# A short convolution on eight 64-row by 32-column tiles, fed by a shifted copy of its input made on chip

## The chip, the cores and the metric

The kernel runs on one core of a Trainium2 chip. The metric is the device time of one execution in microseconds (us), the median of several runs. A run is called slow when it is over 1.5% above the fastest run of the same kernel. Ratios are the mean time of one kernel's fast runs over that of the other's fast runs of the same rounds, so they are not quite the ratio of the medians that are quoted beside them.

The engines are named as in the profile: PE is TensorE (matmuls), PEld its weight loads, DVE is VectorE, ACT is ScalarE, POOL is GpSimd, SP is the engine that only issues DMAs here. "PEclk" is the TensorE clock that was granted, as a share of full speed.

## The reference

```python
# x: (8, 4224, 192), weight: (8 heads, 7 taps)
w = softmax(weight, axis=-1)
y[b, s, h*24:(h+1)*24] = sum_k w[h, k] * x_pad[b, s + k, h*24:(h+1)*24]   # causal, 6 zero rows ahead
h = (y.transpose(0, 2, 1) @ U @ V).transpose(0, 2, 1)                      # mixing over tokens, rank 32
u = y + h
out = u + relu(u @ w_ch1) @ w_ch2                                          # 192 -> 768 -> 192
```

So every output token needs its own input row and the six rows before it, per head, with a small band matrix.

## The kernel before

The input of a batch lies in one tile `x_sb`. Partitions 0 to 63 hold the first half of the batch's 66 blocks of 64 tokens, partitions 64 to 127 the second half; each half has the block ahead of it as well, for the taps that reach back.

```python
    def x_part(b, r, s0, s1):                    # one of four loads of a batch, float32 to bf16, POOL's queue
        blk = NB0 * r + s0 - 1
        return nc.gpsimd.dma_start(
            out=xt[b][HB * r : HB * r + HB, s0:s1, :],
            in_=x[b, blk * HB : (blk + s1 - s0) * HB, :].rearrange("(j p) d -> p j d", p=HB),
        )
    # ...
    def conv(b, h0, nh, rs, engs, k0=0, k1=NT):  # HB = 64, GS = 24 columns of a head
        # ...
        for hh in range(nh):
            h = h0 + hh
            for halo in range(2):                # this block, then the block before it
                for r in rs:
                    for c in range(2):           # even and odd blocks: the two halves of the output
                        st = 1 - halo + c + 2 * k0
                        nc.tensor.matmul(
                            out=pp[r][HB * c : HB * c + HB, ...],
                            lhsT=band[HB * r : HB * r + HB, h, HB * halo : HB * halo + HB],
                            rhs=xt[b][HB * r : HB * r + HB, st : st + 2 * nk[r] - 1 : 2, h * GS : h * GS + GS],
                            start=(halo == 0), stop=(halo == 1),
                            tile_position=(HB * r, HB * c),
                        )
        # ... then one eviction of pp[r] (PSUM) to y_sb for each r, on ACT or DVE
```

A head thus costs eight matmuls on 64x64 tiles and two evictions (128x384 and 128x408). Four run at a time: at the start of a conv in the trace of the kernel before, four start within 10 ns (125.365 to 125.375 us) and the next four 0.18 us later (from 125.551). The second four are the halo products, most of whose band is zero.

The main loop is a row of stretches. Each has W1 (`relu(u @ w_ch1)`, line L518) of three groups of eight token tiles, then the conv of a batch or part of one, then twelve W2 pieces (L542), between which the mixing products for later groups are put (`h`: add the rank-32 part to y; then a DMA transpose `uT` on SP's queue for a later W1).

```python
    CONV = {
        5: [(3, 0, 8)], 6: [(4, 0, 8)], 7: [(5, 0, 4)],
        8: [(5, 4, 8), (6, 0, 3)], 9: [(6, 3, 8), (7, 0, 2)], 10: [(7, 2, 8)],
    }   # stretch: (batch, first head, end)
    # ...
    for gs1, gs2, convs, at in SLOTS:
        for g in gs1:
            ends = w1(g, RELU0 if g < 2 else RELU)
            # ... x loads of a later batch, held back until given W1 products
        for b, h0, h1 in convs:
            for h in range(h0, h1):
                conv(b, h, 1, [0, 1], "AD" if n > 2 else "A")
        for p in range(npc + 1):
            for what in at.get(p, []):
                do(what)                          # h group, its transpose, sums over tokens
            # ... one W2 piece, its eviction on DVE, its output DMA on SP's queue
```

## Time and profile before

| | |
|---|---|
| time | 336.25 us median of 3 (334.5 to 336.35) |
| PE busy | 97% of a span of 332.2 us |
| DVE, ACT busy | 84%, 48% |
| conv of batches 1 to 7 in the chain | 22.3 us, 56 heads |

Three lines of the page of the kernel before: PE's busy time, and over 40 slices of the span the granted clock and the busy share of the DMA engines in tenths.

```profile
PE 323.7 (97%) x4072; PEld 226.9 (68%) x4072; DVE 280.3 (84%) x571; ACT 159.2 (48%) x327; POOL 38.0 (11%) x63
...
PEclk9999999999999999999999999999999999999999
DMA  8999994799999899899699695069049239439135
```

PE is busy for 97% of the span, and the mean granted clock is 1.000.

The chain of waits of the kernel before, one stretch with a conv of eight heads (start, duration, what):

```profile
125.44 3.30 PE ps L309 x61
128.74 2.09 PE ps L542 x24
130.82 0.28 PE ps L424 x8
131.10 4.07 PE ps L542 x48
```

Only PE pieces: the conv (L309) is 3.30 us, on the critical path. The timeline of the same place shows why it is 3.30 and not less:

```profile
125.36 3.37 PE L309 MATMUL ps<-x_sb,band 64*64 64x384 bf16 x64
125.96 3.19 ACT L271 ACTIVATE y_sb<-ps 128x384 bf16<-128x384 f32 x8
126.11 4.00 DVE L273 CAST y_sb<-ps 128x408 bf16<-128x408 f32 x8
```

ACT and DVE evict from start to end, eight times each, about 0.5 us apiece; PE outruns them after five heads and then waits for banks: the last three heads start at 127.226, 127.716 and 128.206 us, each 0.05 us after one of DVE's evictions has ended (127.173, 127.662 and 128.152).

The stretch table of the kernel before, for four stretches (the last column but one is the DMA share: the time of all packets over 16 engines times the stretch; above 1 means that the times of packets overlap):

```profile
core 0: us, PE busy (x) PEld busy (x) DVE busy (x) ACT busy (x) POOL busy (x), PEclk, DMA share, GB/s
113.67:142.88 29.21, 29.21 (x378) 20.24 (x379) 25.42 (x54) 14.64 (x30) 3.53 (x5) 1.00 1.02 182
142.88:169.36 26.48, 26.48 (x311) 18.34 (x312) 23.79 (x46) 12.78 (x25) 3.55 (x5) 1.00 1.09 186
169.36:198.16 28.80, 28.80 (x369) 20.07 (x371) 25.36 (x52) 14.26 (x29) 3.35 (x4) 1.00 1.04 177
198.16:226.96 28.80, 28.80 (x369) 20.10 (x371) 25.68 (x55) 14.26 (x29) 0.00 (x0) 1.00 0.53 137
```

The first three stretches load a batch of x (POOL issues) and have DMA shares of 1.02 to 1.09. The fourth loads none: 0.53.

SP's timeline of the kernel before, near the conv of batch 1, which PE reaches at 40.4 us:

```profile
36.63 2.28 SPq L465 DMA_TRANSPOSE uT<-u_sb  x1
38.95 2.01 SPq L557 DMA_DIRECT2D out_dram<-out_sb  x2
```

### The profile page before, as it was taken

The page shows a single profiled execution, that of the slowest core. Times are in us where ns is not written, and L with a number is a line of the kernel's source. Part 1 is how long each engine was busy: PE and PEld are TensorE (multiplying, and loading weights), DVE is VectorE, ACT ScalarE, POOL GpSimd, SP SyncE. Part 2 cuts the span into 40 slices and gives each one's busy share as a digit, 9 for nine tenths or more (in the row PEclk, how much of TensorE's full clock was granted, in tenths as well). Part 3 has the DMA queues.
Part 4 walks back from the last instruction along what each step waited for, and adds up shares of the span by engine and source line. Part 5 has one row for each costly group of instructions (what it writes and reads, how often), then busy time and mean ns, then how long its engine had stood idle before and what let it go on. Part 6 is the DMA issues. An engine that isn't in the chain of part 4 may idle for free.

```text
span 332.2 us, 9693 instructions
## 1 busy us (share of the span) xinstructions
PE 323.7 (97%) x4072; PEld 226.9 (68%) x4072; DVE 280.3 (84%) x571; ACT 159.2 (48%) x327; POOL 38.0 (11%) x63
## 2 busy tenths in 40 slices
PE   7889999999999999999999999999999999999995
PEld 7745675578559747955965884695597487488495
DVE  5757999989898889899888898889898889887863
ACT  1658436650790295068049209605902921922910
POOL 8471110210210030021012000000000000000000
PEclk9999999999999999999999999999999999999999
DMA  8999994799999899899699695069049239439135
GB/s 102 193 160 186 139 235 118 136 199 256 200 188 134 231 188 166 186 203 199 183 202 194 107 235 139 19 180 234 2 73 278 81 83 255 94 80 251 54 119 169
DMA packets 122909, 53.55 MB, mean 161 GB/s; under 512 B 87760, under 2 KB 122832, under 8 KB 122864
## 3 DMA queue, kind: packets, MB, share of 16 engines
q1 hardware_dynamic: 84672, 38.18, 49.1%
q0 software_dynamic: 38192, 14.73, 39.2%
q8 instruction: 32, 0.52, 0.6%
q14 instruction: 13, 0.11, 0.1%
HBM read 29.49 MB, written 25.95 MB: 167 GB/s over the span
## 4 chain that ended last, share of the span: by engine, by line
PE 88%; DMA 3%; ACT 3%; POOL 2%; DVE 2%; issue 0%; POOLq 0%
PE ps L542 41%; PE ps L518 37%; PE ps L309 6%; PE ps L424 3%; DMA x_sb<-in_x_dram 3%; ACT rl_sb L529 2%; PE ps L339 2%; DVE y_sb L273 1%; DMA V_sb<-in_moe_V_dram 1%; POOL x_sb L78 1%; DVE rl_sb L531 1%; PE ps L395 0%; POOL V_sb L152 0%; DVE uT L273 0%; POOL Ur L129 0%
## 5 line engine op out<-in xcount | busy, mean ns | idle before, releaser
L529 ACT ACTIVATE rl_sb<-ps 128x512 bf16<-128x512 f32 x235 | 125.2, 605 | 104.9 <-PE ps L518 83.6
L542 PE MATMUL ps<-W_sb,rl_sb 128*128 128x192 bf16 x1584 | 138.9, 246 | 0.0
L542 PEld LDWEIGHTS <-rl_sb 128*128 128x128 bf16 x1584 | 128.7, 98 | 8.9 <-issue 8.8
L518 PE MATMUL ps<-uT,W_sb 64*128 64x512 bf16 x1188 | 131.5, 376 | 0.8 <-DVE uT L273 0.8
L531 DVE TENSOR_SCALAR rl_sb<-ps 128x512 bf16<-128x512 f32 x161 | 105.6, 689 | 19.7 <-PE ps L518 19.3
L518 PEld LDWEIGHTS <-W_sb 64*128 64x128 bf16 x1188 | 57.8, 94 | 70.1 <-issue 4.3
L550 DVE TENSOR_TENSOR out_sb<-ps,u_sb 128x384 f32<-128x384 f32 (+1 forms) x133 | 69.5, 548 | 15.8 <-PE ps L542 15.5
L446 DVE TENSOR_TENSOR u_sb<-y_sb,ps 128x192 bf16<-128x192 bf16 (+1 forms) x168 | 66.2, 460 | 0.0
L78 POOL DMA_DIRECT2D x_sb<-in_x_dram x32 | 27.0, 848 | 134.9 <-PE ps L518 123.1
L273 DVE CAST y_sb<-ps 128x408 bf16<-128x408 f32 (+2 forms) x66 | 32.4, 560 | 2.3 <-PE ps L309 2.3
L309 PE MATMUL ps<-x_sb,band 64*64 64x408 bf16 (+4 forms) x576 | 26.8, 313 | 0.2 <-DMA x_sb<-in_x_dram 0.2
L271 ACT ACTIVATE y_sb<-ps 128x384 bf16<-128x384 f32 (+2 forms) x66 | 26.0, 522 | 1.4 <-PE ps L309 1.2
L309 PEld LDWEIGHTS <-band 64*64 64x64 bf16 x576 | 18.0, 106 | 9.1 <-issue 7.4
L353 ACT ACTIVATE tt_hi<-ps 128x192 bf16<-128x192 f32 x7 | 2.3, 330 | 41.1 <-PE ps L339 41.1
L424 PE MATMUL ps<-tt_sb,V_sb 32*128 32x192 bf16 x264 | 12.1, 246 | 0.2 <-DVE y_sb L273 0.2
L172 PE MATMUL ps<-zz 128*128 128x128 bf16 x90 | 7.6, 266 | 1.2 <-DVE zz L167 1.2
L424 PEld LDWEIGHTS <-V_sb 32*128 32x128 bf16 x264 | 4.5, 92 | 6.3 <-issue 5.8
L172 PEld LDWEIGHTS <-zz 128*128 128x128 bf16 x90 | 7.3, 124 | 1.2 <-DVE zz L167 1.2
L339 PE MATMUL ps<-y_sb,U_sb 128*32 128x192 bf16 x257 | 7.2, 247 | 0.0
L339 PEld LDWEIGHTS <-U_sb 128*32 128x32 bf16 x257 | 5.4, 96 | 1.2 <-issue 1.1
L354 DVE TENSOR_TENSOR tt_lo<-ps,tt_hi 128x192 bf16<-128x192 f32 x7 | 2.5, 356 | 3.9 <-ACT tt_hi L353 3.9
L239 ACT ACTIVATE band<-ps 32x152 bf16<-32x152 f32 x8 | 2.3, 288 | 3.1 <-PE ps L230 3.0
(57 smaller groups left out, 45.1 us busy)
## 6 DMA issues: line engine op xcount, KB each, us to landing
out_dram<-out_sb SPq DMA_DIRECT2D x131, 192.0 KB, 2.8
x_sb<-in_x_dram POOLq DMA_DIRECT2D x14, 384.0 KB, 7.9
x_sb<-in_x_dram POOLq DMA_DIRECT2D x7, 432.0 KB, 9.5
x_sb<-in_x_dram POOLq DMA_DIRECT2D x7, 408.0 KB, 9.6
x_sb<-in_x_dram POOLq DMA_DIRECT2D x1, 648.0 KB, 9.5
x_sb<-in_x_dram POOLq DMA_DIRECT2D x1, 624.0 KB, 7.2
uT<-u_sb SPq DMA_TRANSPOSE x31, 4.2
W_sb<-in_moe_w_ch_dram POOLq DMA_DIRECT2D x2, 192.0 KB, 6.3
```

The costliest lines, as they stand in the source:

```text
L78: return nc.gpsimd.dma_start(out=xt[b][HB * r : HB * r + HB, s0:s1, :], in_=x[b, blk * HB : (blk + s1 - s0) * HB, :].rearrange("(j p) d -> ...
L271: nc.scalar.activation(out=out, in_=in_, func=ACT.Copy)
L273: nc.vector.tensor_copy(out=out, in_=in_)
L309: nc.tensor.matmul(out=pp[r][HB * c : HB * c + HB, 0 : nk[r] * w].rearrange("p (k a) -> p k a", a=w)[:, :, hh * GS : hh * GS + GS], lhsT=b ...
L339: nc.tensor.matmul(out=p[32 * c : 32 * c + 32, o : o + D], lhsT=U_sb[:, j // 4, j % 4, :], rhs=yt[b][:, j, :], start=(n < 4), stop=(n + 4 ...
L424: nc.tensor.matmul(out=banks[pr][:, a * D : (a + 1) * D], lhsT=V_sb[32 * q : 32 * q + 32, (j // 8) * 2 + j % 2, :], rhs=ttb[b][32 * q : 32 ...
L446: nc.vector.tensor_tensor(out=u_group(g)[:, i : i + n, :, hf, :], in0=yt[b][:, run[0] : run[0] + n, :].rearrange("p n (c k) -> p n c k", c=3),
L518: last = nc.tensor.matmul(out=pp[hf][:], lhsT=W1_sb[HB * hf : HB * hf + HB, c, m * P : (m + 1) * P], rhs=uTt[g][HB * hf : HB * hf + HB, :, ...
L529: nc.scalar.activation(out=rl[:, m, hf, :], in_=pp[hf][:], func=ACT.Relu)
L531: nc.vector.tensor_scalar_max(out=rl[:, m, hf, :], in0=pp[hf][:], scalar1=0.0)
L542: nc.tensor.matmul(out=cps[:, a * D : (a + 1) * D], lhsT=rlt[g][:, m, hf, (i + a) * P : (i + a + 1) * P], rhs=W2_sb[:, m, :], start=(m == ...
L550: nc.vector.tensor_tensor(out=o[:, 0:n, :].rearrange("p n (c k) -> p n c k", c=3), in0=cps[:, 0 : n * D].rearrange("p (n c k) -> p n c k", ...
```

## The change

Its intent: drop the halo products. If a second tile `xb_sb` holds the same tokens shifted by 32, then 64 rows of either tile hold 32 output tokens together with the 32 tokens before them, so one product with 64 rows and 32 output columns gives them without any halo. `x_sb` gives the odd 32-token blocks, `xb_sb` the even ones. Eight such tiles cover the 128 by 128 that one W2 product takes (128*128 in the profile's forms, 64*32 for these). The shifted tile is made on chip by four DMAs of 32 partitions each, SBUF to SBUF, on SP's queue. The conv is cut into chunks of two or three heads that stand between W2 pieces, so that evictions have time.

```diff
-    xs = ctx.enter_context(tc.tile_pool(name="xs", bufs=3))
+    xs = ctx.enter_context(tc.tile_pool(name="xs", bufs=2))
+    xbs = ctx.enter_context(tc.tile_pool(name="xbs", bufs=1))
...
+    def x_shift(b):
+        xbt[b] = xbs.tile([P, NB1, D], BF16, name="xb_sb")
+        q = [slice(QB * r, QB * r + QB) for r in range(4)]
+        for dst, src, n in ((2, 1, NB0), (0, 3, NB1)):
+            nc.sync.dma_start(out=xbt[b][q[dst], 0:n, :], in_=xt[b][q[src], 0:n, :])
+            nc.sync.dma_start(out=xbt[b][q[dst + 1], 0:n, :], in_=xt[b][q[src - 1], 1 : n + 1, :])
+
+    def conv32(b, h0, nh, engs):
...
+            for c in range(2):
+                for src in range(2):
+                    for r in range(2):
+                        t, o, cg = ((xt[b], 1, 2 * c + 1), (xbt[b], 0, 2 * c))[src]
+                        part = (r, 1 - r)[src]
+                        st = o + c
+                        nc.tensor.matmul(
+                            out=pp[part][QB * cg : QB * cg + QB, 0 : nk[part] * GS],
+                            lhsT=band[HB * r : HB * r + HB, h, QB : 2 * QB],
+                            rhs=t[HB * r : HB * r + HB, st : st + 2 * nk[part] - 1 : 2, hs],
+                            start=True, stop=True,
+                            tile_position=(HB * r, QB * cg),
+                        )
... (two evictions a head, as before; "AAD" is the turn of ACT and DVE)
-        ([1], [0], [], {0: ["h0"], 1: ["h3"]}),
-        ([2], [1], [(1, 0, 8)], {0: ["h1"], 1: ["t1"], 3: ["s1"], 4: ["h4"]}),
+        ([1], [0], {0: ["h0"], 1: ["h3", "x1"]}),           # x1: the shift of batch 1, before W2 piece 1
+        ([2], [1], {0: ["c1:0:3:AAD", "h1"], 1: ["c1:3:3:AD"], 2: ["c1:6:2:AD"],
+                    3: ["t1"], 4: ["s1", "h4", "x2"]}),
... (batches 2 and 3 likewise)
+        elif k < 10:                                       # stretches 6 to 9, batches 4 to 7
+            hp = (5, 8, 11)
+            put(0, f"c{k - 2}:0:2:AAD")
+            put(1, f"c{k - 2}:2:3:AD")
+            put(2, f"c{k - 2}:5:3:AD")
+            put(8, f"s{k - 2}")
...
+        if k < 9:
+            put(12, f"x{k - 1}")                           # the next batch's shift, at the stretch's end
```

More of the change, by code (lines that the diff above doesn't have):

```diff
@@ L293, in u_layout @@
             )
+    xbt = [None] * B
+    def x_shift(b):
[5 more added lines that the diff above has]
+    def conv32(b, h0, nh, engs):
+        if yt[b] is None:
+            yt[b] = ys.tile([P, NT, D], BF16, name="y_sb")
+        nk = (NB0 // 2, NB1 // 2)
+        for n in range(nh):
+            h = h0 + n
+            hs = slice(h * GS, h * GS + GS)
+            pp = [bank(), bank()]
+            for c in range(2):
[8 more added lines that the diff above has]
+                            rhs=t[HB * r : HB * r + HB, st : st + 2 * nk[part] - 1 : 2, hs],
+                            start=True,
+                            stop=True,
+                            tile_position=(HB * r, QB * cg),
+                        )
+            for part in range(2):
+                j0 = NB0 // 2 * part
+                evac(
+                    engs[(2 * n + part) % len(engs)],
+                    yt[b][:, j0 : j0 + nk[part], hs],
+                    pp[part][:, 0 : nk[part] * GS].rearrange("p (k a) -> p k a", a=GS),
+                )
     def conv(b, h0, nh, rs, engs, k0=0, k1=NT):
@@ L387, in tt_done @@
     def tt_done(b, p):
-        t = sml.tile([P, D], BF16, name="tt_sb")
+        t = sml.tile([P, D], BF16, name="tt_sb", bufs=3)
         nc.vector.tensor_copy(out=t[:], in_=p[:, 0:D])
@@ L570 @@
     SLOTS = [
-        ([0], [], [], {}),
-        ([1], [0], [], {0: ["h0"], 1: ["h3"]}),
-        ([2], [1], [(1, 0, 8)], {0: ["h1"], 1: ["t1"], 3: ["s1"], 4: ["h4"]}),
-        ([3], [2], [(2, 0, 4)], {1: ["h5"]}),
+        ([0], [], {}),
+        ([1], [0], {0: ["h0"], 1: ["h3", "x1"]}),
+        (
+            [2],
+            [1],
+            {
+                0: ["c1:0:3:AAD", "h1"],
+                1: ["c1:3:3:AD"],
+                2: ["c1:6:2:AD"],
+                3: ["t1"],
+                4: ["s1", "h4", "x2"],
+            },
+        ),
+        ([3], [2], {1: ["h5"]}),
         (
@@ L577 @@
             [3, 4, 5],
-            [(2, 4, 8)],
-            {1: ["t2", "h6"], 3: ["s2"], 4: ["h7"], 7: ["h8"], 10: ["h9"]},
-        ),
-    ]
-    CONV = {
-        5: [(3, 0, 8)],
-        6: [(4, 0, 8)],
-        7: [(5, 0, 4)],
-        8: [(5, 4, 8), (6, 0, 3)],
-        9: [(6, 3, 8), (7, 0, 2)],
-        10: [(7, 2, 8)],
-    }
-    SUMS = {5: (3, 5), 6: (4, 10), 8: (5, 2), 9: (6, 6), 10: (7, 10)}
+            {
+                0: ["c2:0:2:AAD"],
+                1: ["c2:2:3:AD", "h6"],
+                2: ["c2:5:3:AD"],
+                4: ["t2", "h7"],
+                6: ["s2"],
+                7: ["h8"],
+                10: ["h9"],
+                12: ["x3"],
+            },
+        ),
+    ]
     nh = 10
@@ L594, with put @@
         at = {}
-        for p in (1, 5, 9) if k == 5 else (2, 6, 10):
+        def put(p, *what):
+            at.setdefault(p, []).extend(what)
+        if k == 5:
+            hp = (6, 9, 11)
+            put(0, "c3:0:3:AD")
+            put(2, "c3:3:3:A")
+            put(7, "c3:6:2:AAD")
+            put(11, "s3")
+        elif k < 10:
[4 more added lines that the diff above has]
+            put(8, f"s{k - 2}")
+        else:
+            hp = (0, 4, 8)
+        for p in hp:
             if nh < NG:
-                at.setdefault(p, []).append(f"h{nh}")
+                put(p, f"h{nh}")
                 nh += 1
-        if k in SUMS:
-            b, p = SUMS[k]
-            at.setdefault(p, []).insert(0, f"t{b}")
-            at.setdefault(p + 2, []).insert(0, f"s{b}")
-        SLOTS.append((gs, gs, CONV.get(k, []), at))
+        if k < 10:
+            put(hp[k == 5], f"t{k - 2}")
+        if k < 9:
+            put(12, f"x{k - 1}")
+        SLOTS.append((gs, gs, at))
     assert nh == NG
-    LOADS = {2: [(1, 5), (1, 5), (2, 2), (2, 5)]}
-    for b, g in ((3, 4), (4, 6), (5, 9), (6, 12), (7, 15)):
+    LOADS = {2: [(1, 5), (1, 5), (2, 2), (2, 5)], 3: [(4, 1), (4, 4), (5, 1), (5, 4)]}
+    for b in range(4, B):
+        g = 3 * b - 6
         LOADS[b] = [(g, 1), (g, 4), (g + 1, 1), (g + 1, 4)]
-    def held(ins, after):
-        tc.add_manual_dep(
-            ins.ins,
-            after.ins.name,
-            mybir.DependencyInfo(mybir.DependencyClass.Sync, mybir.DependencyReason.DATA),
-            reason="load held back",
-        )
     idle(30, P)
@@ L641, in do @@
     def do(what):
+        if what[0] == "c":
+            b, h0, n, engs = what[1:].split(":")
+            conv32(int(b), int(h0), int(n), engs)
+            return
         n = int(what[1:])
@@ L646, in do @@
                 transp(n)
+        elif what[0] == "x":
+            x_shift(n)
         elif what[0] == "t":
@@ L650, in do @@
             tt_sum(n)
-    for gs1, gs2, convs, at in SLOTS:
+    for gs1, gs2, at in SLOTS:
         for g in gs1:
@@ L664 @@
                 do("h2")
-        n = sum(h1 - h0 for _, h0, h1 in convs)
-        for b, h0, h1 in convs:
-            for h in range(h0, h1):
-                conv(b, h, 1, [0, 1], "AD" if n > 2 else "A")
         npc = 4 * len(gs2)
```

## The prediction

> **What bounds the kernel now.** TensorE. The page's busy table has PE at 97%, DVE 84%, ACT 48%. From 33 us on the chain of waits is an almost unbroken run of PE pieces: W2 (L542) 41% of the span, W1 (L518) 37%, conv (L309) 6%. W2 costs 0.083 us per matmul, W1 0.109. So saved PE time is saved time, unless a new wait replaces it.
>
> **What the conv costs.** Batches 1 to 7 are 56 heads. In the chain, four heads take 1.50 us, eight take 3.30; the pieces add up to about 22.3 us. The timeline shows about 0.345 us per head while banks are free (8 matmuls, 43 ns each), then 0.49 per head, because DVE needs 0.572 us for each 128x408 eviction and ACT 0.535 for 128x384.
>
> **What the change removes.** The halo products are half of the array work. [...] Nearest in this trace is the four-column product with U: 33 matmuls in 0.85 us, 26 ns each. Eight at that rate is 0.21 us per head, 11.5 us for 56. Each of 21 chunks pays perhaps 0.12 us to enter and 0.06 on the next W2 piece: 3.5 us together, about 0.5 of it paid before. Conv gain: about 8 us. Evictions are as many and as large; DVE loses one a batch (7 of 16).
>
> **What it adds.**
> 1. Seven shifts of 1.6 MB on SP's queue. Later ones have a W1 stretch (11.8 us) to land in, and should just fit. The first has not: it comes after the transpose that SP issues at 36.6 us and holds for 2.3, so no earlier than 38.9 us, while the conv of batch 1 is reached at 40.4. The DMA row is full there and transfers take 6.9 us to land: landing about 45 to 48 us, an estimate. PE must stand still some 5 us (3 to 8), once, on the critical path.
> 2. The sum for batch 1 now directly precedes the h group that needs it, no W2 piece between; the same for batch 3. With DVE behind by a microsecond or two: about 1.5 us for both.
> 3. In stretches of three groups with a conv, DVE works 26.4 of 29.3 us now. Shorter by 1.3 us, with nearly the same DVE work and an h group just before W1, late evictions will hold banks: about 0.4 us in each of five, 2 us.
>
> **Sum.** -8 + 5 + 1.5 + 2 = about 0.5 us. I predict 335.8 us, range 328 to 343. Chance faster by over 2%: 0.20; within 2%: 0.65; slower by over 2%: 0.15.
>
> **What would show it.** Still eight conv matmuls per head, but with starts about 26 ns apart instead of 43. One PE idle gap of several us near 40 us, released by the shift's DMA. Small PE gaps at W1 starts and before the h groups of batches 1 and 3, released by DVE. DVE share unchanged or higher.
>
> **What would make it wrong.** If the first shift lands by 42 us, the result is nearer 331. [...] If later shifts are late too, several more stalls, above 343.

No term of the sum is cut; it stands at about 0.5 us, and the 0.21 us per head rests on the 26 ns of the products with U. The terms are estimates. The 0.12 us to enter a chunk is 1.50 us for four heads less four times 0.345. The 0.06 us on the next W2 piece, the 1.5 us and the 2 us are guesses that no trace shows; beside the last stands DVE's 26.42 us of work in the 29.28 us from 84.39 us.

## The result, and the profile after

The changed kernel took 397.58 us (median of 4, 397.45 to 405.75; the last of them slow), against 336.29 us for the kernel before (median of 4). The ratio is 1.184, with a 95% interval of 1.179 to 1.189: 18% slower. The prediction of 335.8 us, range 328 to 343, was wrong.

The page after, the lines that answer to those of before:

```profile
PE 329.5 (83%) x4072; PEld 222.8 (56%) x4072; DVE 276.4 (70%) x561; ACT 165.5 (42%) x337; POOL 37.9 (10%) x63
...
PEclk9999759968999699979968997999999999999999
DMA  9999984998799969998999899699384792927425
```

PE fell from 97% to 83% of the span, and the clock row has six dips.

PE's waits after (who waited for whom: us in total, times, the longest):

```profile
PE ps L324 <- DMA xb_sb<-x_sb: 44.3, 6, 13.1
PE ps L562 <- DMA uT<-u_sb: 11.9, 1, 11.9
PE ps L468 <- DVE tt_sb L433: 1.3, 3, 0.6
```

Nothing like the first two lines was there before. Six of the seven convs waited for their shift, 44.3 us in all, in order 13.1, 6.7, 5.5, 8.9, 7.6 and 2.6; and one W1 (L562) waited 11.9 us for a transpose that SP issued right behind a shift, at 74.8 us, and that landed 14.0 us later. Two loads of x ran beside it.

The chain of waits after, through one shift (pieces left out are waits of under 0.1 us and SP's output issue):

```profile
150.61 2.09 PE ps L562 x18
152.71 0.28 SPq L509
...
153.81 0.54 SPq L305
...
154.41 0.59 SPq L306
...
155.11 1.72 SPq L305
...
156.87 11.21 DMA xb_sb<-x_sb
...
168.13 0.87 PE ps L324 x11
```

W1 begins at 150.61 and takes 11.8 us. The shift's first piece is issued only at 153.81, since SP waits for the last output and transpose; the fourth is issued at 156.87 and lands 11.2 us later, at 168.1. PE is ready for it at 162.3.

The stretch table after, from W1 start to W1 start, for the stretches that answer to the four shown of before:

```profile
core 0: us, PE busy (x) PEld busy (x) DVE busy (x) ACT busy (x) POOL busy (x), PEclk, DMA share, GB/s
150.60:186.80 36.20, 30.72 (x378) 20.14 (x379) 24.98 (x52) 15.38 (x31) 3.52 (x5) 0.91 1.06 178
186.80:225.57 38.77, 29.86 (x378) 19.61 (x379) 25.57 (x52) 15.39 (x31) 3.53 (x5) 0.87 1.13 178
225.57:263.05 37.48, 29.88 (x378) 19.57 (x379) 25.57 (x51) 15.39 (x31) 3.35 (x4) 0.91 1.05 183
263.05:293.93 30.88, 28.30 (x378) 18.89 (x379) 25.57 (x55) 15.38 (x31) 0.00 (x0) 1.00 0.73 169
```

Multiply the length of a stretch by its DMA share, and one has the DMA time that it holds. Before it was 29.8, 28.9 and 30.0 us for the three stretches with x loads, about as much as the stretches were long. After it is 38.4, 43.8 and 39.4 us, and the stretches grew by 7.0, 12.3 and 8.7 us. The fourth stretch, without a load, had 15.3 us and got 22.5, and grew by 2.1. (Overlapping packets are counted twice in such a product; it is a load and not a capacity.)

The DMA issues after (count, size, median us from issue to landing), first the shift's pieces, then loads of x:

```profile
xb_sb<-x_sb SPq DMA_DIRECT2D x14, 408.0 KB, 11.1
xb_sb<-x_sb SPq DMA_DIRECT2D x14, 384.0 KB, 8.0
x_sb<-in_x_dram POOLq DMA_DIRECT2D x7, 432.0 KB, 15.6
x_sb<-in_x_dram POOLq DMA_DIRECT2D x7, 408.0 KB, 16.6
```

The same loads before:

```profile
x_sb<-in_x_dram POOLq DMA_DIRECT2D x7, 432.0 KB, 9.5
x_sb<-in_x_dram POOLq DMA_DIRECT2D x7, 408.0 KB, 9.6
```

The loads became 6 to 7 us later as well: both sides lose.

Where the 63.5 us between the two spans (332.2 and 395.7) went, worked out from the trace's records: PE's idle time after 30 us grew by 57.6 us. The granted clock fell to 0.5 in the six gaps of 5.5 us or more and stayed there past their ends; PE was busy for 23.5 us at half clock, so about 11.7 us went there, an estimate. The rest, 5.8 us the other way, is what PE's shorter work saved.

### The profile page after: what moved, and what is told of

Its sections match the earlier page's. It is cut to its first block, busy times and chain, and to the rows that moved or that the text cites. A ratio compares the mean times of both kernels' runs of the same rounds, so it can differ in the third digit from the quotient of the medians.

```text
span 395.7 us, 9752 instructions
## 1 busy us (share of the span) xinstructions
PE 329.5 (83%) x4072; PEld 222.8 (56%) x4072; DVE 276.4 (70%) x561; ACT 165.5 (42%) x337; POOL 37.9 (10%) x63
## 4 chain that ended last, share of the span: by engine, by line
PE 58%; DMA 23%; DVE 10%; SPq 4%; issue 2%; ACT 2%; POOL 0%; DVEq 0%; POOLq 0%
PE ps L586 32%; PE ps L562 18%; DMA xb_sb<-x_sb 17%; PE ps L324 4%; DMA uT<-u_sb 4%; DVE u_sb L490 3%; SPq L305 3%; DMA x_sb<-in_x_dram 3%; DVE out_sb L594 2%; DVE rl_sb L575 2%; PE ps L468 2%; PE ps L383 2%; ACT rl_sb L573 1%; SPq L306 1%; DVE y_sb L274 1%
## 5 line engine op out<-in xcount | busy, mean ns | idle before, releaser
L586 PE MATMUL ps<-W_sb,rl_sb 128*128 128x192 bf16 x1584 | 145.9, 252 | 0.1
L562 PE MATMUL ps<-uT,W_sb 64*128 64x512 bf16 x1188 | 132.7, 379 | 12.6 <-DMA uT<-u_sb 11.9
L586 PEld LDWEIGHTS <-rl_sb 128*128 128x128 bf16 x1584 | 133.0, 100 | 14.8 <-issue 14.0
L562 PEld LDWEIGHTS <-W_sb 64*128 64x128 bf16 x1188 | 58.0, 95 | 83.0 <-DMA uT<-u_sb 12.4
L274 DVE CAST y_sb<-ps 128x408 bf16<-128x408 f32 (+2 forms) x56 | 28.3, 555 | 49.3 <-PE ps L324 46.5
L272 ACT ACTIVATE y_sb<-ps 128x384 bf16<-128x384 f32 (+3 forms) x76 | 31.4, 492 | 66.9 <-PE ps L324 64.8
L324 PE MATMUL ps<-xb_sb,band 64*32 64x384 bf16 (+1 forms) x224 | 16.9, 396 | 44.3 <-DMA xb_sb<-x_sb 44.3
L324 PEld LDWEIGHTS <-band 64*32 64x32 bf16 x448 | 5.8, 97 | 53.1 <-DMA xb_sb<-x_sb 44.0
L324 PE MATMUL ps<-x_sb,band 64*32 64x384 bf16 (+1 forms) x224 | 19.3, 388 | 0.1
L468 PE MATMUL ps<-tt_sb,V_sb 32*128 32x192 bf16 x264 | 13.9, 249 | 1.4 <-DVE tt_sb L433 1.3
L74 POOL MEMSET x_sb<- 64x96 uint32 x7 | 1.3, 190 | 78.3 <-PE ps L324 73.1
```

Source lines behind the costliest of these rows:

```text
L272: nc.scalar.activation(out=out, in_=in_, func=ACT.Copy)
L274: nc.vector.tensor_copy(out=out, in_=in_)
L324: nc.tensor.matmul(out=pp[part][QB * cg : QB * cg + QB, 0 : nk[part] * GS], lhsT=band[HB * r : HB * r + HB, h, QB : 2 * QB], rhs=t[HB * r ...
L468: nc.tensor.matmul(out=banks[pr][:, a * D : (a + 1) * D], lhsT=V_sb[32 * q : 32 * q + 32, (j // 8) * 2 + j % 2, :], rhs=ttb[b][32 * q : 32 ...
L562: last = nc.tensor.matmul(out=pp[hf][:], lhsT=W1_sb[HB * hf : HB * hf + HB, c, m * P : (m + 1) * P], rhs=uTt[g][HB * hf : HB * hf + HB, :, ...
L586: nc.tensor.matmul(out=cps[:, a * D : (a + 1) * D], lhsT=rlt[g][:, m, hf, (i + a) * P : (i + a + 1) * P], rhs=W2_sb[:, m, :], start=(m == ...
```

## The experiments

Twelve kernels ran. Several give wrong results, to take one thing away.

### 1. No shift at all

```diff
-        # four shift DMAs
+        return
...
-    t, o, cg = ((xt[b], 1, 2 * c + 1), (xbt[b], 0, 2 * c))[src]
+    t, o, cg = ((xt[b], 1, 2 * c + 1), (xt[b], 0, 2 * c))[src]
```

(The block index of the second source is clipped as well, to stay inside loaded data.)

> The changed kernel without any shift; the second half of each head reads the unshifted tile instead (wrong result on purpose). Theory 1 (the conv gained what was hoped, and the whole loss is the shifts): no wait for a shift, none of 11.9 us for uT, clock 1.0 from start to end, span near 327 us, that is 8 to 10 us under the kernel before; a chunk of three heads costs about 0.64 us. Rival (denser DVE and bank holding cost as well): PE gaps at W1 starts, and a time of 332 us or more.

Measured: 330.02 us (4 runs) against 334.44 (7 runs), ratio 0.9865 (0.985 to 0.988). Wrong result. No wait for uT, no gap before W1. The chain of this run in a stretch with a conv of eight heads:

```profile
126.28 0.47 PE ps L320 x10
126.74 1.10 PE ps L582 x12
127.84 0.64 PE ps L320 x17
```

A chunk of two heads (L320) takes 0.47 us, of three 0.64: 0.17 us per head, 21 ns per matmul on average, and about 0.13 to enter. So eight tiles do run at once (in the trace of the changed kernel, the eight matmuls of a head start within 23 ns, 170.964 to 170.987 us), and the three chunks (the third is like the second) cost 1.75 us where the conv of eight heads took 3.30. But the gain was 4.4 us, not 8 to 10. From the starts of the stretches: stretches 6 to 10, with batches 4 to 7 and 32 heads in both kernels, take 136.5 us instead of 141.5 (5.0 less, 1.26 a batch). From the W1 of group 2 to stretch 6 it took 77.5 us instead of 77.1: batches 1 to 3 gained nothing.

The two traces show where that gain went, if PE's time is summed from the start of each piece to the start of the next. Up to stretch 6 the conv fell from 9.6 to 6.5 us, but the mixing products `h` rose from 3.5 to 6.5. Five of the ten `h` pieces take 0.88 to 1.16 us, where the other five take 0.34: three follow the sum over tokens that they need (one with a W2 piece between), two stand directly behind a conv chunk. In stretches 6 to 10 every `h` takes about 0.34, and all together they cost 4.4 us in both kernels. Over both parts the conv fell by 8.9 us, the W2 pieces grew by 0.8, and `h` took 3.0 back.

This run has the changed kernel's two buffers for x in place of three and its order of work, so neither by itself explains the 18%. Its second stretch is a warning about the DMA share (columns as in the stretch tables): 1.26, and PE was busy throughout.

```profile
142.38:170.32 27.94, 27.94 (x377) 18.70 (x379) 25.37 (x52) 15.28 (x31) 3.53 (x5) 1.00 1.26 189
```

### 2. The shifts land unread

The edit is that of experiment 1 for the matmul's source, with the four DMAs kept.

> As the run without shifts, but the four shift DMAs of each batch are issued and land unread (wrong result on purpose). Theory 1 (the loss is PE waiting for the landing, then running at half clock): within 3 us of the run without shifts, unless the uT wait near 75 us stays, which would be 12 us and some half clock more. Rival (the extra 11.3 MB crowd out transposes, loads and outputs): clearly slower than without shifts, 345 us or more, with PE waits for uT or x_sb in several stretches.

Measured: 358.62 us, ratio 1.0712 (1.069 to 1.074). 28.6 us more than without shifts, though no conv waits. So theory 1 fell in its strict form: traffic alone costs much. PE's waits in this run:

```profile
PE ps L562 <- DMA uT<-u_sb: 16.1, 4, 10.9
PE ps L562 <- DVE out_sb L594: 3.7, 2, 2.8
PE ps L586 <- DVE out_sb L594: 3.4, 2, 2.4
```

The first line is W1 waiting for transposes. The other two name DVE's output addition, and that in its turn waited 10.2 us for output tiles whose DMAs had not landed. Of the 67.6 us between 330.0 and 397.6, then, 28.6 are traffic and 39.0 the waiting for the landings, half clock included in both. (The kernel before took 336.3 us in the changed kernel's rounds and 334.4 in these, so the 39.0 is good to about 2 us.)

### 3. Two pieces on another queue

```diff
-        for dst, src, n in ((2, 1, NB0), (0, 3, NB1)):
-            nc.sync.dma_start(...)
+        for dst, src, n, eng in ((2, 1, NB0, nc.sync), (0, 3, NB1, nc.scalar)):
+            eng.dma_start(...)
```

> The changed kernel with the last two of the four shift pieces issued from ACT's queue instead of SP's. [...] Theory A [...]: both pairs run side by side, and the last shift, which has no x load beside it, takes 4 to 5 us from first to last landing instead of 5.8 after the first; the four pieces land within about 6 us of issue instead of 10. Theory B (16 DMA engines, each with big packets, are the limit): no shorter in total. Time 375 to 392 us under A, about 397 under B.

(Theory A here and in experiment 4 is that a piece of 32 partitions has a limit of its own.) The code leaves on SP the two pieces from partitions 0 to 63 to 64 to 127, and gives ACT the two that go the other way.

Measured: 409.47 and 419.55 us, correct; the second is slow, and it is the one profiled. Inconclusive between the theories: the pieces on ACT's queue were issued long before SP's (the last pair at 273.4 against 294.3 us), so the two pairs never ran side by side. ACT's pieces met transposes instead and landed up to 15.3 us after issue. Nothing in these two runs shows that a second queue bought room.

### 4. One copy over 128 partitions

```diff
-        # four DMAs of 32 partitions
+        nc.sync.dma_start(out=xbt[b][:, 0 : NB0 + 1, :], in_=xt[b][:, 0 : NB0 + 1, :])
+        nc.sync.dma_start(out=xbt[b][0:HB, NB0 + 1, :], in_=xt[b][0:HB, NB0, :])   # one last block
```

> The same bytes copied as one DMA over all 128 partitions, unshifted (wrong result on purpose). Theory A [...]: packets of about 13 KB take near 0.5 us instead of 0.9, and the copy is through in about 4 to 5 us from issue where nothing else runs (the last one), against 9.9 us from first issue to last landing in the changed kernel; stalls shrink, time 360 to 375 us. Theory B (big packets or the engines themselves are slow): packets still 0.9 us, 7 to 8 us of transfer, time 385 us or more.

Measured: 363.28 us (fast) and 378.96 us (slow, and profiled), wrong result. In the trace's records of single packets, the median of the big packets is 487 ns, against 934 ns in the changed kernel. The time lies in theory A's range, 34 us under the changed kernel. It is still 29 us over the kernel before (334.4), so the slow pieces are not the whole loss.

### 5. The four pieces, each in place

```diff
+        for r, n in ((2, NB0), (3, NB0), (0, NB0 + 1), (1, NB0 + 1)):
+            nc.sync.dma_start(out=xbt[b][q[r], 0:n, :], in_=xt[b][q[r], 0:n, :])
```

(With the same small DMA for a last block as in experiment 4.)

> The changed kernel with its four DMAs of 32 partitions each, but every piece copied to the partitions it came from (wrong result on purpose; one small DMA fills a last block). The copy over 128 partitions had packets of 0.49 us, the shift 0.9; the two differed in the span of a piece and in crossing from one group of partitions to another. If the span of 32 partitions is what halves the rate, packets stay near 0.9 us, the pieces land some 1.9 us apart and the time is 390 us or more. If the crossing is, packets take 0.5 us, the pieces land about 1 us apart and the time is 360 to 380 us.

Measured: 400.56 us (2 fast runs), packets of 926 ns at the median, the last four pieces landing 1.85, 1.97 and 1.82 us apart. So the span of 32 partitions halves the rate, not the crossing.

| | big packet, median | the last shift, first to last packet | rate |
|---|---|---|---|
| changed kernel, four pieces of 32 | 934 ns | 7.46 us for 1.62 MB | 217 GB/s |
| pieces of 32 in place (5) | 926 ns | 7.29 us for 1.60 MB | 219 GB/s |
| one copy of 128, unread (6, below) | 487 ns | 4.01 us | 404 GB/s |

Each is the last shift of its run, with no x load beside it; the others took 8.3 to 11.3 us in the changed kernel and 5.2 to 7.2 us in experiment 6, whose profile is of a slow run. Why a span of 32 partitions halves the rate was not shown.

### 6. Unread, but over 128 partitions

Experiment 2 with the copy of experiment 4.

> The unread traffic again, but as one copy over 128 partitions of the same bytes, at the old places (wrong result on purpose); packets took 0.49 us there instead of 0.9. If the 28.6 us that unread shifts cost come from the time that they hold the queue, about half should go: 340 to 348 us. If bytes count, 355 to 360 us as before.

Measured: 334.29 us (fast) and 341.86 us (slow, and profiled). Against the 330.0 us without shifts that is 4.3 us in the one fast run, 11.8 in the slow one, not 28.6. The same bytes cost a fraction once they hold the engines for about half the time (4.01 us for the last shift, against 7.46). With experiment 4 this splits the loss at the full rate as well: 4.3 us of traffic and 29.0 of waiting for the landings (one fast run each), against 28.6 and 39.0 with pieces of 32. (The two were measured on two chips, with 334.6 and 334.4 us for the kernel before.)

Over 100 us in the middle of the profiled run, slow as it was, the DMA share was 1.31 and PE was busy for 98.57 us:

```profile
100.00:200.00 100.00, 98.57 (x1310) 65.86 (x1305) 86.62 (x172) 58.50 (x120) 12.32 (x17) 1.00 1.31 227
```

In experiment 2 the same 100 us have a share of 1.26, and PE was busy for 92.9 us of them. So the share does not tell the two apart. They differ in the pieces: packets of 487 ns at the median here, of 954 ns there.

### 7. The shifts earlier

```diff
-                7: ["h8"],
-                12: ["x3"],
+                7: ["h8", "x3"],
...
-            put(12, f"x{k - 1}")
+            put(8 if k == 5 else 7, f"x{k - 1}")
```

> The changed kernel with the shifts of batches 3 to 6 (and 7) issued four or five W2 pieces earlier in their stretch, where the loads should have landed; the shifts of batches 1 and 2 stay. Theory 1 (the shift takes 8 to 10 us from its first issue wherever it stands, and it was issued too late): the five waits from 131 us on, 31.3 us together, fall to under 5 us and the half clock after them goes; the wait near 54 us (13 us) and the uT wait near 89 us stay; time 355 to 367 us. Rival (the queues are so full that a shift moved forward makes the transposes and outputs behind it late instead): as many us come back as waits of W1 for uT, time above 375 us.

Measured: 397.90 us (2 runs), correct: no gain at all. PE's waits:

```profile
PE ps L562 <- DMA uT<-u_sb: 37.7, 5, 11.9
PE ps L324 <- DMA xb_sb<-x_sb: 13.8, 2, 13.0
```

The rival was right. The convs of batches 3 to 7 no longer wait for their shifts (0.7 us is left), but W1 now waits for the transposes behind them, 25.8 us more than in the changed kernel. Moving the load about does not make room for it.

### 8. No x loads from batch 3 on

```diff
+        xt[b] = xt[b] or xt[b - 2]      # in x_shift
-    LOADS = {2: [...], 3: [...]}  and batches 4 to 7
+    LOADS = {2: [(1, 5), (1, 5), (2, 2), (2, 5)]}
```

> The changed kernel, shifts and waits as they are, but the x loads of batches 3 to 7 left out; old tiles are used again (wrong result on purpose). Theory (in the stretches with x loads the 16 DMA engines were already full, so every shift of 8 to 9 us lengthens its stretch by about that): without loads there is room, the waits for shifts from 100 us on fall from 31.3 us to under 8, the wait for uT near 89 us goes too, the wait near 54 us stays; 345 to 358 us. Rival (the shift is late by its place and its own 10 us, whatever else runs): waits stay above 15 us, time 370 us or more.

Measured: 364.01 us (2 fast runs), wrong result. PE's waits:

```profile
PE ps L325 <- DMA xb_sb<-x_sb: 23.2, 6, 12.8
PE ps L563 <- DMA uT<-u_sb: 3.9, 1, 3.9
```

The waits for shifts after 100 us are 10.4 us instead of 31.3, and the uT wait is 3.9 instead of 11.9. That is somewhat over the 8 us and the 358 us that the theory allowed, and far from the rival's 15 us. So two thirds of those waits come from the x loads beside the shifts. The 10.4 us left are the shift's place: without x loads it is issued 3.6 to 4.8 us into an 11.8 us W1 and needs 9.6 to 10.1 us from its first issue to its last landing, 2 us too much each time. A gap of 2.05 us, from 116.64 us, was followed by a lower clock as well: 3.40 us from 119.10 us at a granted 0.51. The gap of 2.58 us in the changed kernel, from 275.1 us, was not: 1.00 behind it.

The packet records show how the loads do it. In the changed kernel the first packet of the shifts that meet a load (3 to 6) moves 4.2 to 6.6 us after the first issue, here 1.2 to 1.3 us; the transfer itself takes 8.3 to 9.2 us there, 7.6 to 8.0 here. Over shifts 3 to 7, first issue to last landing is 20.3 us longer in total in the changed kernel: 14.8 us are the later start, 4.5 the slower transfer. So most of what the loads add is the time before the shift's first packet. For shift 4, issued at 153.8, packets of the x load held 0.56 to 0.99 of the 16 engines from 154.5 to 156.5 us, the output that SP had issued ahead of it at 153.1 landed only at 158.3, and its own first packet moved at 158.1.

### 9 and 10. Batches 4 to 7 alone, on SP's queue and on POOL's

Both keep the kernel before's order up to batch 3, and issue the shifts early. They differ in one word, `nc.sync` or `nc.gpsimd` for the four pieces.

> The order of the kernel before up to batch 3 (64x64 tiles, halo products); only batches 4 to 7 by the new conv, their shifts issued early on SP. In the run without shifts the stretches of batches 4 to 7 were 5.05 us shorter than before, and the ones up to batch 3 not shorter at all. Theory 1: this keeps that 5 us and pays little: 329 to 332 us, faster than both kernels. Rival (shift traffic costs even where nothing waits for it: about 9 of the waits in the run with unread shifts fell after 140 us): 333 to 340 us, waits of W1 for uT in the stretches of batches 4 to 6.

> The same, with the four shift pieces issued from POOL's queue, where the x loads are, instead of SP's, where the transposes and outputs are. If the shift's cost is that transposes stand in line behind it on one queue, the waits for uT of the SP version go and this is 329 to 331 us. If it is that the shared engines are held by the big packets whichever queue they come from, it is no faster than the SP version.

Measured: on SP's queue 360.60 us, ratio 1.077 (1.074 to 1.079). On POOL's queue 347.82 us in the one fast run, 355.63 to 360.34 in three slow ones. Both correct. The SP version lost 25.4 us to waits of W1 for uT (15.0, 8.9 and 1.5). The POOL version still waits for uT, 14.5 us in four places in its slow profiled run. Neither expectation was met: the fast run is 12.8 us under the SP version, so the place in SP's queue may be a part of the cost, but that rests on one run. The 14.5 us of uT waits stood behind shifts that are not in the transposes' queue: another queue alone did not spare the transposes, as far as a slow run can show. Neither version comes near 336 us.

### 11. Batches 6 and 7 alone

The kernel before with the new conv for the two batches whose shifts come after the last x load; batch 5 on the old conv, whole.

```diff
-        7: [(5, 0, 4)], 8: [(5, 4, 8), (6, 0, 3)], 9: [(6, 3, 8), (7, 0, 2)], 10: [(7, 2, 8)],
+        7: [(5, 0, 8)],
+        # 8: {12: x6}, 9: {0, 1, 2: c6, 3: x7}, 10: {0, 1, 2: c7}
```

> The kernel before, with the new conv for batches 6 and 7 alone, whose shifts start after the last x load has been issued, at the end of one stretch and early in the next; batch 5 keeps the old conv, whole. If the engines have room there, nothing waits: the stretches add up to 2.3 us less than before, 332 us, a ratio near 0.993. If a shift costs even there, W1 waits for uT or a conv chunk for its shift and the time is 335 us or more.

Measured: 339.08 us (6 runs) against 335.91 (11 runs), ratio 1.0098 (1.007 to 1.013), correct. Even in the quiet part it is 1% slower. The shift of batch 6 was issued 4 us into its W1 again (203.3 for 199.2) and PE waited 1.7 us for it. Beside the shift of batch 7, W1 took 13.8 us in place of 11.8: it waited for banks, while DVE stood still for 4.3 us for an output tile. The output that SP issued behind the shift at 229.0 landed 5.9 us later; the two before the shift had taken about 2. The two stretches with the new conv took 30.9 and 30.6 us, where the run without shifts had 27.9. So no version was found that beats the kernel before.

### 12. No shift, evictions of batches 1 to 3 on ACT

Experiment 1 with "A" for every eviction of those batches.

> The run without shifts again (wrong result on purpose), with all evictions of batches 1 to 3 on ACT. In the run without shifts these batches gained nothing over the kernel before, and the chain there ran over DVE pieces. If DVE was what held them, taking 4 us of evictions a batch off it brings 2 to 4 us: 326 to 328 us. If it was the banks or the order of the chunks, no change or slower: 330 us or more.

Measured: 331.78 us, ratio 0.988 (0.984 to 0.992), the same as experiment 1 within the intervals (0.985 to 0.988). Taking DVE's evictions away brought nothing: the `h` pieces up to stretch 6 cost 7.1 us here, 6.5 in experiment 1. The chain before them is a mix of short DVE and ACT pieces. So the time goes where an `h` piece stands close behind a conv chunk or the sum that it needs, and neither engine alone is shown to be the cause. No run moved the `h` pieces.

## Why the prediction was wrong

- **The step that failed** is in point 1 of "What it adds": "Later ones have a W1 stretch (11.8 us) to land in, and should just fit." They did not. Five more convs waited, 31.3 us in all. Their shifts were issued 3.3 to 5.1 us into that W1, behind SP's outputs and transpose, and took 9.9 to 15.8 us from first issue to last landing. Two things were missed. First, the shift was taken as "1.6 MB" with no time of its own. Four pieces of 32 partitions run at 217 GB/s, 7.5 us with next to nothing beside them, and experiments 4 and 5 show that their span is the reason. Even without x loads this is 2 us too late each time (experiment 8). Second, the loads of x stand in the same place. Beside them a shift starts and moves later, which makes two thirds of the waits (experiment 8), and a shift put elsewhere delays the transposes instead (experiments 2 and 7). The stretch table before showed where the loads stand, but not this cost.
- **The first wait** was predicted in the right place and for the right reason (behind the transpose of 36.6 us, no earlier than 38.9 us), but was 13.1 us where 5 (3 to 8) was said. The first piece was issued at 39.56, the last landed at 54.3 instead of 45 to 48: 14.7 us from first issue to last landing, with two loads of x beside it. The 6.9 us that the prediction took for a landing was a transpose's (issued at 36.63 us in the trace before, landed 6.86 later).
- **What was not in the sum at all:** the transpose behind a shift and beside loads of x (11.9 us; 3.9 without the loads; the slowest transpose took 14.0 us to landing where it took 9.3 before, while the median went from 4.2 to 4.0), and the half clock after each of the six gaps of 5.5 us or more (about 11.7 us, the estimate above). The traffic effect on other DMAs was thought of only for the shift itself.
- **The conv gain** was put at 8 us. It was right: experiment 1 has 8.9 us less conv and 0.8 more W2. The matmuls were better than assumed, 0.17 us per head for 0.21. The whole gain of experiment 1 is only 4.4 us, mostly because of the next term.
- **The sums that precede their h group** were put at 1.5 us. The place was right and the size too small: the three waits for `tt_sb` are 1.3 us, but with the `h` pieces behind a conv chunk, which the prediction did not name, `h` costs 3.0 us more in experiment 1.
- **DVE holding banks at W1 starts**, 2 us, did not show: experiment 1 has no PE gap there.
- **Two row groups writing one bank at once** cost nothing that shows: row groups 0 and 64 write different quarters of the partitions of one bank in the same eight matmuls, which start within 23 ns (170.964 to 170.987 us); the results are correct and a head takes 0.17 us.
- "If later shifts are late too, several more stalls, above 343" named the actual outcome among the ways to be wrong, but gave it too little weight, and its size was not worked out.

What stays open: how the later start of a shift beside x loads divides between engines held by the load and SP's own transfers ahead of it; whether two opposite pairs of pieces side by side would reach the 404 GB/s of one copy over 128 partitions (experiment 3 did not get them side by side); and whether other places for the `h` pieces would keep the gain of batches 1 to 3.

## What to carry to other kernels

Work that is taken off a busy engine and given to DMA has to land in time and hold up no other transfer. Here it did neither: of 67.6 us lost 28.6 were traffic and 39.0 the waiting for the landings. Add it up from the moment at which the queue can issue it to the last landing, in the stretch where it will stand: here 13.9 to 15.8 us beside loads of x, 9.6 to 10.1 without. Time a transfer by the partitions it spans and not by its bytes alone (217 GB/s in pieces of 32 here, 404 in one copy of 128), and ask which later transfers stand behind it. A DMA share near 1 says that transfers will meet; whether that costs PE anything has to be tried, as by landing the same bytes unread: at the same share of 1.26, PE was busy for all of 27.94 us in experiment 1 and for 92.9 of 100 us in experiment 2. When a delayed transfer is cured by moving it and the same microseconds come back as waits for another transfer (25.8 us of them in experiment 7), the load is the cause and not the place alone.
